# Banded attention into a squared-ReLU FFN on one core: first-batch order and idle matmuls, and the row order of the first second-layer tile

## The chip, the cores and the metric

The kernel runs on one core of one Trainium2 chip. Its engines work side by side, each through its own list of instructions in order: PE (TensorE, matrix multiplication; PEld is its weight load), DVE (VectorE) and ACT (ScalarE) for element-wise work, POOL (GpSimd), which here only issues DMA loads, and SP (SyncE), which issues stores and transposing DMAs. An engine that meets an instruction whose input isn't ready waits, and all that stands behind it in its list waits too.

The metric is device time in microseconds (us). The time of the kernel is the median of several executions; a profile shows one execution, with a span from its first to its last instruction. PEclk in a profile is the share of its full clock that TensorE was granted.

## What is computed

Eight batches of eight heads with 576 tokens and 64 channels go through causal attention within a narrow set of keys, and the 4608 rows that come out (512 wide) through a two-layer FFN whose activation is a squared ReLU.

```python
scores = (1/sqrt(64)) * q @ k^T
rel = pos[:, None] - pos[None, :]
mask_plain = (rel >= 0) & (rel < 32)                      # heads 0 to 3
mask_dil   = (rel >= 0) & (rel < 128) & (rel % 4 == 0)    # heads 4 to 7
attn = softmax(where(mask, scores, -1e9))
x = (attn @ v).transpose(0, 2, 1, 3).reshape(8 * 576, 512)
out = square(maximum(x @ w_in, 0)) @ w_out                # 512 -> 2048 -> 512
```

q, k, v and the weights arrive as float32 and are turned to bf16 by the DMAs that load them. The output is float32.

## The kernel before

**Tiles.** Heads go in four pairs, e = 0 and 1 for the plain mask, 2 and 3 for the dilated one. A batch is cut into two parts of 64 and 80 columns (times 4 residues, so 256 and 320 tokens). The attention output, transposed, lies in `xT`. The FFN takes it in tiles of 512 tokens, the first 1024 tokens as four half tiles of 256. For a half tile `ffn_groups` gives eight first-layer groups (`g1`; eight matmuls of 256 columns each, L665, then a ReLU on ACT, L676, and a square on DVE, L677) and two row blocks of four second-layer groups (`g2`; four matmuls of 512 columns each, L697). Part p of a row block needs rows of chunk p of `w_out`; after part 3 the block is copied from PSUM to an output buffer `osb` on ACT (L703; three such buffers) and stored by SP (L639). Chunk c of `w_in` serves first-layer groups 2c and 2c + 1 of each half tile.

**Buffers in PSUM.** `ps_f` ("pf") has four buffers, `ps_a` ("pa") two, `ps_o` and `ps_d` one each. A batch's transposes and scores go to "pa". The values' product and its row sums go to `po` and `pd`, or, for odd pairs of batches 0 and 1, to two "pa" buffers in part 0 and two "pf" buffers in part 1.

**The order of work** is written out by hand. `PROGRAM` (L21) is a string of codes between bars: all before the first bar runs before the first FFN group, and what stands behind bar number g + 1 runs after group g. The list `groups` gives the order of the FFN groups (L801, L802): the first layer of half tiles 0 and 1 in 16 groups, then their second layer, part by part over all four row blocks. So the four blocks hold all four "pf" buffers until part 3. The codes that matter here:

- `L0:...` a load on POOL's queue: `L0:q001` queries and keys of batch 0, part 0, pairs 0 and 1; `L0:v0d`, `L0:v0p`, `L0:v1r` values (L184, L178, L197); `L0:i0` to `i3` chunks of `w_in` (L751); `L0:o0` to `o3` chunks of `w_out` (L756). POOL issues them in order, and each waits for the transfer eight places ahead of it to land.
- `w22`, `W3`: so many idle matmuls (256 and 128 columns, L465) on a cleared tile. They compute nothing that is used.
- For batch 0, with pair e and part p: `Tep` transposes of queries and keys on PE (L493), `Cep` copies out of PSUM on DVE or ACT (L500 to L508), `Bep` the mask added by matmuls (L534), `Sep` scores (L553), `Eep` exponentials on ACT (L558), `Pep` values (L584), `Dep` row sums (L600), `Lep` and `Xep` the reciprocal by logarithm and exponential on ACT (L607, L610), `Mep` the product into `xT` on DVE (L617). In part 0 a pair of pairs shares one P, D, L, X and M step (`P20 P30`, then one `M20`).
- `z` and `y` clear buffers of later batches on DVE (L714, L715, L769, L770).
- For later batches: `1q1`, `1Q1` transposes of batch 1's queries for part 0 and part 1 with their copies (L235, L248), `1k1` keys (L252, L259), `1a1`, `1b1` scores (L304, L310, L314, L315), `1o1`, `1p1` values and outputs (L413 to L428), `1v2` spreading of values (L207).

The step that transposes in the first batch and the idle matmuls:

```python
if what == "T":
    ps = ps_a.tile([P, 1024], bf16, name="pa")
    first["T", e, part] = x = ps[:, 0 : 2 * w].rearrange("p (x r m) -> p x r m", x=2, r=RES)
    for z, nm in enumerate("qk"):
...
def turn(n: int, cols: int):
    if "W" not in first:
        pool, nm = (ps_f, "pf") if ("P", 2, 0) in first else (ps_o, "po")
        first["W"] = pool.tile([P, 512], f32, name=nm)
```

Of the kernel before, what the change touches and what calls it, by code (L numbers as in the profile page):

```python
# [12 lines left out]
RES = 4  # L13
# [6 lines left out]

PROGRAM = (  # L21
    "L0:q001 L0:q023 L0:q101 L0:q123 L0:v0d L0:v0p L0:i0 L0:v1d L0:i1 L0:v1p L0:v1r L0:i2 L0:i3 L0:o0 "
    "L1:q00123 L0:o1 L0:o2 w22 T00 C00a T10 C10a B00 B10 S00 E00 T20 C20v S10 E10 T30 C30v B20 B30 S20 E20 W3 "
    "S30 E30 W4 T01 C01v T11 C11v B01 B11 W4 S01 E01 T21 C21v W3 S11 E11 T31 C31v B21 B31 P20 P30 D20 D30 W3 "
    "S21 E21 L20 X20 W3 S31 E31 M20 W4 P00 P10 D00 D10 L00 X00 M00 | | P21 P31 D21 D31 L21 X21 M21 L31 X31 M31 "
    "| | P01 P11 D01 D11 L01 X01 M01 L11 X11 M11 | | | | | | | | | | | | z | | y L1:v0dp L0:o3 L1:q10123 "
    "L1:v1dpr | | | | L2:q00123 L2:q10123 1q1 1q3 | 1q2 | 1k2 | 1k1 1v3 | 1a2 | 1v2 1k0 1q0 | 1o2 | 1a0 1a1 | "
    "1k3 1o0 1o1 | 1a3 1Q0 | 1K0 1o3 | 1Q1 1K1 | 1Q2 | 1b0 | | 1Q3 1K2 L2:vwpdr L3:q00123 L3:q10123 | L2:x | | "
    "2q0 | | 2k0 1V2 | 1b2 1p0 | 1b1 1V3 1K3 | | 1p2 1p1 | 2a0 1b3 | 2k1 2o0 2b0 1p3 | 2q1 2k2 L3:x | | 2q2 "
    "2p0 L3:vwpdr 2a1 | | | 2b1 | 2v2 2o1 2q3 2a2 | | 2p1 | 2k3 | 2b2 2o2 | 2v3 | 2a3 2p2 L4:q10123 | 2b3 | "  # L30
    "3k1 2o3 3q1 | | 3a1 L4:q00123 2p3 | 3k0 3k2 | | 3o1 | | | 3q0 3v2 | | | | 3a0 | 3b1 3k3 | | | 3p1 L4:x "
    "3q2 L4:vwpdr | | 3b0 | 3a2 3q3 3o0 4k0 | | | 3o2 3b2 | | 3p0 3v3 | 4q1 3a3 | 3p2 4q2 4q0 | L5:q10123 3b3 "
    "| 3o3 | 4k1 | | L5:q00123 3p3 4k2 4k3 4a0 L5:vwpdr | | | 4b0 | | 4q3 | | 4o0 | | | 4a2 4v2 | 4b2 | 4a3 "
    "L5:x 4a1 | 4o2 | | | 4p2 L6:q00123 4v3 | | 4b1 | | 4p0 | | 4p1 | 5q0 5k0 | 4b3 | | | | 4o1 | | 5k2 "
    "L6:q10123 4o3 | 5q2 5k1 | | 4p3 | 5q1 |"
)

# [26 lines left out]
def kernel(  # L64
# [10 lines left out]
    P = nc.NUM_PARTITIONS  # L75
# [4 lines left out]
    bf16 = mybir.dt.bfloat16  # L80
# [20 lines left out]
    NF = DFF // P  # L101
# [9 lines left out]
    ps_f = ctx.enter_context(tc.tile_pool(name="ps_f", bufs=4, space=bass.MemoryType.PSUM))  # L111
    ps_a = ctx.enter_context(tc.tile_pool(name="ps_a", bufs=2, space=bass.MemoryType.PSUM))
# [37 lines left out]
    def staged(b: int, nm: str):  # L150


        t = rb[STAGE[b]][nm]
        return t[:, :].rearrange("p (a h x) -> p a h x", h=H, a=2)
# [47 lines left out]
    def spread_v(b: int, e: int, parts):  # L202

        p0, p1 = parts[0], parts[-1] + 1
        for hl in range(2):
            rows = slice(64 * hl, 64 * hl + 64)
            nc.vector.tensor_copy(  # L207
                vbd[b % 2][rows, e, RES * p0 : RES * p1, rows],
                vds[b][rows, e - NE // 2, p0:p1, :].rearrange("p m (r d) -> p (m r) d", d=D),
            )  # L210
# [10 lines left out]
    def trans(b: int, e: int, nm: str, part: int):  # L221

        ps = ps_a.tile([P, 1024], bf16, name="pa")
        t = staged(b, nm)
        copy = nc.scalar.copy if nm == "q" and e < NE // 2 else nc.vector.tensor_copy
        if b == 2:
            m0, n, pitch, cuts = 0, M, M, [(t[0:80, a, :, :], MS[a], 80) for a in range(2)]
        else:

            m0, n, pitch, cuts = MS[part], MN[part], 80, [(t[0:80, part, :, :], 0, 80)]  # L230
        pv_ = ps[:, 0 : 4 * pitch].rearrange("p (h c m) -> p h c m", h=2, c=2)
        for hl in range(2):
            for c in range(2):
                for src, c0, w in cuts:
                    nc.tensor.transpose(  # L235
                        pv_[:, hl, c, c0 : c0 + w], src[:, 2 * e + hl, P * c : P * c + P], ident[0:w, 0:w]
                    )
        halves(e, nm, pv_[:, :, :, 0:n], m0, n, copy)

    def halves(e: int, nm: str, t, m0: int, n: int, copy):  # L240


        for hl in range(2):
            rows = slice(64 * hl, 64 * hl + 64)
            for jj in range(2):
                src = t[64 * jj : 64 * jj + 64, hl, :, :]
                if nm == "q":
                    copy(  # L248
                        qT[rows, e, :, m0 : m0 + n].rearrange("p (c j) m -> p j c m", j=2)[:, jj, :, :], src
                    )  # L250
                elif e < NE // 2:
                    copy(  # L252
                        kbd[rows, e, m0 // 16 : (m0 + n) // 16, rows].rearrange(
                            "p i (m c j) -> p j i m c", c=2, j=2)[:, jj, :, :, :],
                        src.rearrange("p c (i m) -> p i m c", m=16),
                    )
                else:
                    x0, x1 = m0 // 64, min((m0 + n) // 64, 2)
                    copy(  # L259
                        kbd[rows, e, RES * x0 : RES * x1, rows].rearrange(  # L260
                            "p (x c j) m -> p j c x m", c=2, j=2)[:, jj, :, :, :],
                        src[:, :, 0 : 64 * (x1 - x0)].rearrange("p c (x m) -> p c x m", m=64),
                    )
                    if m0 + n == M:
                        copy(
                            kbd[rows, e, 8, rows].rearrange("p (m c j) -> p j m c", c=2, j=2)[:, jj, :, :],
                            src[:, :, n - 16 : n].rearrange("p c m -> p m c"),
                        )
# [163 lines left out]
    def step(b: int, code: str):  # L432

        what, e = code[0], int(code[1])
        part = int(what in "QKVbp")
        if what in "qk" and (b > XB or b == XB and e >= NE // 2):
            t = (qx if what == "q" else kx)[b % 2]
            by_act = what == "q" and e < NE // 2 and b < ADDED  # L440
            halves(
                e, what, t[:, 2 * e : 2 * e + 2, :, :], 0, M, nc.scalar.copy if by_act else nc.vector.tensor_copy
            )
        elif what in "qQkK":
            trans(b, e, what.lower(), part)
        elif what in "vV":
            spread_v(b, e, [part] if b in PARTED else [0, 1])
        elif what in "ab":
            scores(b, e, part)
        elif b in PARTED and e % 2:  # L450
            pv(b, e, part, *((ps_f, "pf") if part else (ps_a, "pa")))
        else:
            pv(b, e, part)

    first = {}
# [13 lines left out]
    def first_step(code: str):  # L469
# [5 lines left out]
        what, e, part = code[0], int(code[1]), int(code[2])  # L475
# [3 lines left out]
        w = RES * n  # L479
# [3 lines left out]
        def byr(ap):  # L483
            return ap.rearrange("p (r m) -> p r m", r=RES)

        if what == "T":
            ps = ps_a.tile([P, 1024], bf16, name="pa")
            first["T", e, part] = x = ps[:, 0 : 2 * w].rearrange("p (x r m) -> p x r m", x=2, r=RES)
            for z, nm in enumerate("qk"):
                t = staged(0, nm)  # L490
                for r in range(RES):
                    for hl, rows in enumerate(sides):
                        nc.tensor.transpose(  # L493
                            x[rows, z, r, :], t[0:n, part, 2 * e + hl, D * r : D * r + D], ident[0:n, 0:n]
                        )
        elif what == "C":
            copy = nc.scalar.copy if code[3] == "a" else nc.vector.tensor_copy
            x = first.pop(("T", e, part))
# [13 lines left out]
        elif what == "B":  # L512
# [11 lines left out]
            else:  # L524
                i0, x = (4, 32) if part else (3, 0)
# [9 lines left out]
        elif what == "S":  # L535
            ps = first["S", e, part]
# [3 lines left out]
            y = 0  # L540
            for x, (i, r, q0, q1) in enumerate(bl):
                z = (q1 - q0) * (RES if r is None else 1)
# [13 lines left out]
        elif what == "E":  # L556
            ps = first.pop(("S", e, part))
            nc.scalar.activation(pts[e][:, c : c + ps.shape[1]], ps, ACT.Exp, scale=SCALE)  # L558
        elif what == "P":
# [8 lines left out]
            o3, d3 = byr(o), byr(d)  # L568
            pt = pts[e]
            bl = blocks(0, e, part)  # L570
            y, dms = c, []
            for x, (i, r, q0, q1) in enumerate(bl):
                z = (q1 - q0) * (RES if r is None else 1)
# [216 lines left out]
    G = 2 * NF  # L790
# [5 lines left out]
    groups, steps = [], []  # L796
# [2 lines left out]

    head = groups[:G]  # L800
    groups[:NF] = [head[y] for y in (0, 1, 2, 3, 16, 17, 18, 19, 4, 5, 20, 21, 6, 7, 22, 23)]  # L801
    groups[NF:G] = [head[y + part] for part in range(4) for y in (8, 12, 24, 28)]  # L802
    for b in range(5, B):
        at = {"a": (-2, 8), "b": (0, 8), "o": (3, 8), "p": (6, 8), "v": (-4, 8)}
        at = {**({"k": (-9, 4), "q": (-9, 4)} if b > 5 else {}), **at}
# [50 lines left out]
```

## Time and profile before

| what | value |
|---|---|
| time, median of 8 runs | 321.14 us |
| all runs | 319.63 to 322.77 us |
| profiled execution, its time | 322.51 us |
| profiled execution, its span | 320.7 us |
| mean granted TensorE clock | 0.984 |
| PE busy | 307.5 us, 96% of the span |
| DVE busy | 201.2 us, 63% |
| ACT busy | 193.8 us, 60% |
| PE busy in 0 to 10, 20 to 30, 50 to 60, 60 to 70 us | 7.74, 7.82, 8.81, 8.11 us |
| first-layer matmul (256 columns, mean) | 326 ns over all forms |
| second-layer matmul (512 columns, mean) | 373 ns |

The profile gives, for each engine, the time in which it was busy. Matmuls are pipelined: each record is longer than the distance to the next one's start, so counts are turned into time by the distance between starts. The chain of waits follows the last instruction back to whatever released it, step by step. The list of waits sums, for each waiting instruction, how long its engine stood idle and which engine or transfer ended the wait. Where a buffer's earlier reader ended the wait, that reader is named.

### The profile page before, as it was taken

How to read it: one execution, taken by the hardware profiler on the slowest of the kernel's cores; microseconds unless marked ns; L12 is line 12 of the kernel's file. 1: busy time of each engine (PE TensorE's matmuls, PEld its weight loads, DVE VectorE, ACT ScalarE, POOL GpSimd, SP SyncE). 2: the span in 40 equal slices, each digit the busy share in tenths (PEclk: the TensorE clock that was granted, in tenths of full speed). 3: DMA queues.
4: the chain of work that ended last, by engine and by line, in shares of the span. 5: the costliest groups of instructions: out<-in, count | busy, mean ns of one | idle time of the engine just before them, and what ended most of it. 6: DMA issues, size and time to landing. Idle time of an engine off the chain costs nothing.

```text
span 320.7 us, 6834 instructions
## 1 busy us (share of the span) xinstructions
PE 307.5 (96%) x2594; PEld 191.7 (60%) x2594; DVE 201.2 (63%) x641; ACT 193.8 (60%) x416; POOL 87.3 (27%) x136
## 2 busy tenths in 40 slices
PE   7979999699999999999999999999999999999995
PEld 5758944486965555555569855555555555445543
DVE  6324578488896987997589748974897325203400
ACT  6246724676987976587468745874587456316511
POOL 8864279423426234700183032000000000000000
PEclk9589999999999999999999999999999999999999
DMA  8999999999989979998489995802200210031021
GB/s 114 159 175 192 192 163 124 206 142 164 153 88 183 172 115 179 114 181 140 64 118 126 155 128 107 157 9 64 70 1 0 68 66 2 7 91 33 2 65 65
DMA packets 79808, 34.91 MB, mean 109 GB/s; under 512 B 49824, under 2 KB 74784, under 8 KB 79776
## 3 DMA queue, kind: packets, MB, share of 16 engines
q0 software_dynamic: 47680, 18.36, 51.3%
q1 hardware_dynamic: 31952, 15.93, 25.7%
q8 instruction: 20, 0.33, 0.4%
q10 hardware_dynamic: 144, 0.20, 0.2%
q14 instruction: 12, 0.10, 0.1%
HBM read 36.90 MB, written 9.44 MB: 144 GB/s over the span
## 4 chain that ended last, share of the span: by engine, by line
PE 82%; ACT 6%; DVE 5%; DMA 4%; issue 2%; POOL 1%; SPq 0%; ACTq 0%; POOLq 0%
PE pf L665 35%; PE pf L697 34%; PE po L413 3%; PE pd L415 2%; DMA out_dram<-osb 2%; DMA kb<-in_k_dram 2%; PE pa L304 2%; ACT h2T L676 1%; PE pa L310 1%; PE pa L493 1%; DVE kbd L252 1%; ACT rec L607 1%; PE pf L553 1%; PE pf L534 1%; ACT osb L703 1%
## 5 line engine op out<-in xcount | busy, mean ns | idle before, releaser
L665 PE MATMUL pf<-xT,w_in 128*128 128x256 bf16 (+1 forms) x768 | 133.7, 326 | 2.8 <-DVE xT L617 2.5
L697 PE MATMUL pf<-w_out_sb,h2T 128*128 128x512 bf16 (+1 forms) x592 | 134.7, 373 | 0.5 <-ACT osb L703 0.5
L665 PEld LDWEIGHTS <-w_in 128*128 128x128 bf16 x768 | 82.4, 114 | 38.3 <-issue 3.7
L676 ACT ACTIVATE h2T<-pf 128x512 bf16<-128x512 f32 x144 | 83.6, 597 | 26.5 <-PE pf L665 25.7
L697 PEld LDWEIGHTS <-h2T 128*128 128x128 bf16 x592 | 54.2, 98 | 53.7 <-issue 0.7
L677 DVE TENSOR_TENSOR h2T<-h2T 128x512 bf16<-128x512 bf16 x144 | 58.0, 423 | 40.5 <-ACT h2T L676 39.0
L703 ACT COPY osb<-pf 128x512 f32<-128x512 f32 (+1 forms) x37 | 21.2, 572 | 42.5 <-PE pf L697 40.3
L178 POOL DMA_DIRECT2D vbd<-in_v_dram x40 | 28.3, 723 | 64.3 <-PE pd L415 55.1
L428 DVE TENSOR_TENSOR xT<-po,rec 128x288 bf16<-128x288 f32 (+2 forms) x52 | 23.7, 456 | 30.8 <-ACT rec L418 30.2
L417 ACT ACTIVATE rec<-pd 128x288 f32<-128x288 f32 (+2 forms) x52 | 21.5, 413 | 23.7 <-PE pd L415 22.9
L314 ACT ACTIVATE pt<-pa 128x352 bf16<-128x352 f32 (+6 forms) x56 | 27.6, 500 | 10.2 <-PE pa L310 6.3
L418 ACT ACTIVATE rec<-rec 128x288 f32<-128x288 f32 (+2 forms) x56 | 24.8, 444 | 1.8
L413 PEld LDWEIGHTS <-vbd 128*128 128x128 bf16 x286 | 17.0, 97 | 10.6 <-issue 1.3
L248 DVE COPY qT<-xx 64x288 bf16<-64x288 bf16 x80 | 20.1, 251 | 1.1
L161 POOL DMA_DIRECT2D qb<-in_q_dram x18 | 13.0, 722 | 23.7 <-DMA xx<-qb 19.9
L252 DVE COPY kbd<-xx 64x288 bf16<-64x288 bf16 x40 | 18.8, 470 | 0.6
L413 PE MATMUL po<-pt,vbd 128*128 128x96 bf16 (+3 forms) x263 | 18.0, 198 | 0.6 <-DVE xT L428 0.3
L191 POOL DMA_DIRECT2D vd<-in_v_dram x24 | 14.7, 640 | 6.8 <-DMA qb<-in_q_dram 3.7
L415 PE MATMUL pd<-pt,mk 128*128 128x96 bf16 (+5 forms) x158 | 16.3, 204 | 0.0
L161 POOL DMA_DIRECT2D kb<-in_k_dram x18 | 12.8, 713 | 0.5 <-PE pa L310 0.5
L415 PEld LDWEIGHTS <-mk 128*128 128x128 bf16 x204 | 11.6, 97 | 1.8 <-DVE kbd L252 1.1
L304 PE MATMUL pa<-qT,kbd 128*128 128x96 bf16 (+2 forms) x146 | 12.2, 201 | 0.5 <-ACT qT L248 0.5
(85 smaller groups left out, 235.9 us busy)
## 6 DMA issues: line engine op xcount, KB each, us to landing
out_dram<-osb SPq DMA_DIRECT2D x18, 128.0 KB, 3.2
qb<-in_q_dram POOLq DMA_DIRECT2D x7, 320.0 KB, 8.2
kb<-in_k_dram POOLq DMA_DIRECT2D x7, 320.0 KB, 8.7
vd<-in_v_dram POOLq DMA_DIRECT2D x32, 64.0 KB, 4.8
w_in<-in_moe_w_in_dram POOLq DMA_DIRECT2D x4, 512.0 KB, 6.9
w_out_sb<-in_moe_w_out_dram POOLq DMA_DIRECT2D x4, 512.0 KB, 10.5
qb<-in_q_dram POOLq DMA_DIRECT2D x7, 256.0 KB, 5.8
kb<-in_k_dram POOLq DMA_DIRECT2D x7, 256.0 KB, 7.1
```

The costliest lines, as they stand in the source:

```text
L161: nc.gpsimd.dma_start(t[0:n, part, hs, :], src[b, hs, t0 : t0 + RES * n, :].rearrange("h (p r) d -> p h (r d)", r=RES))
L178: nc.gpsimd.dma_start(dst[rows, e, i0:i1, rows], v[b, 2 * e + hl, 64 * i0 : 64 * i1, :].rearrange("(i p) d -> p i d", p=64),)
L314: nc.scalar.activation(pt[:, off : off + n], ps[:, 0:n], ACT.Exp, scale=SCALE)
L413: nc.tensor.matmul(oo, vb[:, e, i, :], rh, start=(x == 0), stop=(x == len(mms) - 1), skip_group_check=True)
L415: nc.tensor.matmul(dd, ones[:, :], rh, start=(x == 0), stop=(x == len(dms) - 1), skip_group_check=True)
L418: nc.scalar.activation(rec[:, 0:n], rec[:, 0:n], ACT.Exp, scale=-1.0)
L428: nc.vector.tensor_tensor(out=tok, in0=o if o is o3 else o[:, 0:n], in1=rec if o is o3 else rec[:, 0:n], op=ALU.mult)
L665: nc.tensor.matmul(acc[u][:, nt * x + y0 : nt * x + y1], w_in_sb[piece][:, kt, c0 : c0 + 509 : 4], xT[:, kt, t0 : t0 + y1 - y0], start=(kt ...
L676: nc.scalar.activation(hv, acc[u][:, :].rearrange("p (x n) -> p x n", x=per), ACT.Relu)
L677: nc.vector.tensor_tensor(out=hv, in0=hv, in1=hv, op=ALU.mult)
L697: nc.tensor.matmul(cur[m][:, c0:c1], h2[:, f, P * m : P * m + P], w_out_sb[:, f, c0:c1], start=(f == 0), stop=(f == NF - 1),)
L703: nc.scalar.copy(osb[:, c0:c1], cur[m][:, c0:c1])
```

## The change

Three edits.

1. The hand-written order of the first batch. Idle matmuls: 2 before `S00`, 3 before `S10`, 14 before the transposes of the second half's queries, 9 between those and the keys' transposes (so `T20` is split in `T20q` and `T20k`), 3 before `S20`, 3 before `S30`, 2 before `S01`, 8 at the end; those of the old order after the opening `w22` (24 in seven places) go. The value steps `P20 P30 D20 D30` and `P00 P10 D00 D10`, with their L, X and M steps, stand ahead of part-1 steps (`T21 S11 T31 S21 S31`) that they followed. The load of the last chunk of `w_out` (`L0:o3`) moves from behind batch 1's first values to right behind `L0:o2`.
2. Values of odd pairs of batches 0 and 1 that go through `pv` use two "pf" buffers in both parts.
3. The second layer of the first two half tiles goes row block by row block: all four parts of a block, then the next block. What stands between the bars of `PROGRAM` stays at the same group numbers.

```diff
 PROGRAM = (
     "L0:q001 L0:q023 L0:q101 L0:q123 L0:v0d L0:v0p L0:i0 L0:v1d L0:i1 L0:v1p L0:v1r L0:i2 L0:i3 L0:o0 "
-    "L1:q00123 L0:o1 L0:o2 w22 T00 C00a T10 C10a B00 B10 S00 E00 T20 C20v S10 E10 T30 C30v B20 B30 S20 E20 W3 "
-    "S30 E30 W4 T01 C01v T11 C11v B01 B11 W4 S01 E01 T21 C21v W3 S11 E11 T31 C31v B21 B31 P20 P30 D20 D30 W3 "
-    "S21 E21 L20 X20 W3 S31 E31 M20 W4 P00 P10 D00 D10 L00 X00 M00 | | P21 P31 D21 D31 L21 X21 M21 L31 X31 M31 "
-    "| | P01 P11 D01 D11 L01 X01 M01 L11 X11 M11 | | | | | | | | | | | | z | | y L1:v0dp L0:o3 L1:q10123 "
+    "L1:q00123 L0:o1 L0:o2 L0:o3 w22 T00 C00a T10 C10a B00 B10 W2 S00 E00 W3 S10 E10 W14 T20q W9 T20k C20v T30 "
+    "C30v B20 B30 W3 S20 E20 W3 S30 E30 T01 C01v T11 C11v B01 B11 W2 S01 E01 P20 P30 D20 D30 T21 C21v S11 L20 "
+    "X20 E11 T31 C31v M20 B21 B31 P00 P10 D00 D10 L00 X00 M00 S21 E21 S31 E31 W8 | | P21 P31 D21 D31 L21 X21 "
+    "M21 L31 X31 M31 | | P01 P11 D01 D11 L01 X01 M01 L11 X11 M11 | | | | | | | | | | | | z | | y L1:v0dp "
+    "L1:q10123 L1:v1dpr | | | | L2:q00123 L2:q10123 1q1 1q3 | 1q2 | 1k2 | 1k1 1v3 | 1a2 | 1v2 1k0 1q0 | 1o2 | "
...
         elif b in PARTED and e % 2:
-            pv(b, e, part, *((ps_f, "pf") if part else (ps_a, "pa")))
+            pv(b, e, part, ps_f, "pf")
...
         if what == "T":
-            ps = ps_a.tile([P, 1024], bf16, name="pa")
-            first["T", e, part] = x = ps[:, 0 : 2 * w].rearrange("p (x r m) -> p x r m", x=2, r=RES)
-            for z, nm in enumerate("qk"):
+            if code[3:] != "k":
+                ps = ps_a.tile([P, 1024], bf16, name="pa")
+                first["T", e, part] = ps[:, 0 : 2 * w].rearrange("p (x r m) -> p x r m", x=2, r=RES)
+            x = first["T", e, part]
+            for z, nm in [(z, nm) for z, nm in enumerate("qk") if code[3:] in ("", nm)]:
...
     groups[:NF] = [head[y] for y in (0, 1, 2, 3, 16, 17, 18, 19, 4, 5, 20, 21, 6, 7, 22, 23)]
-    groups[NF:G] = [head[y + part] for part in range(4) for y in (8, 12, 24, 28)]
+    groups[NF:G] = head[8:16] + head[24:32]
```

The rest of the order that the diff rewraps is the same on both sides.

## The prediction

> **What bounds the kernel now.** I went from the summary to the stretches in which TensorE (PE) is not full, then to the chain of waits, then to the queue that brings the weights.
>
> From 105 us on PE is busy 194.96 of 195 us, so a microsecond won before that stays won. All that the change can earn or lose lies in the first 105 us. The busy times by stretch over the start (columns: stretch, length, then busy us and instructions of PE, its weight load, VectorE (DVE), ScalarE (ACT), POOL; then granted clock, DMA share, GB/s):
>
> ```profile
> 5.13:8.54 3.41, 2.21 (x71) 1.59 (x70) 1.81 (x5) 1.99 (x7) 3.08 (x5) 1.00 1.21 149
> 8.54:11.96 3.42, 3.42 (x71) 2.43 (x63) 0.85 (x2) 1.23 (x3) 2.60 (x4) 0.50 1.46 165
> ...
> 22.20:25.61 3.41, 2.16 (x29) 1.80 (x29) 1.05 (x2) 1.47 (x4) 3.41 (x7) 1.00 1.14 171
> ```
>
> The clock is full at first, falls to half at 8.54 and comes back at 18.78. The stretch before the fall holds two PE waits: 0.35 us for a copy, and 0.85 us for the second half's keys. PE is full in the cold 10.24 us, so they cost up to 5.1 us of PE time.
>
> The chain that ended last, in order of time (start, length, what):
>
> ```profile
> 31.75 8.80 PE pf L665 x79
> ...
> 43.11 1.02 DVE vbd L715
> ...
> 53.47 0.88 PE pf L697 x4
> 54.35 0.02 issue
> 54.37 0.58 ACT osb L703
> ...
> 55.60 6.53 DMA out_dram<-osb
> ...
> 62.23 0.59 ACT osb L703
> ...
> 64.36 1.31 PE pf L665 x12
> ```
>
> After the first layer of the first two half tiles (L665) the chain runs through DVE's clearing and copies for batch 1, and then through a store: all four row blocks of the second layer end together, three output buffers are full, and the fourth copy waits for a store of 6.53 us. What waits of PE and ACT there (waiter, what it waited for, total, times, longest):
>
> ```profile
> PE pa L415 <- DVE kbd L252: 1.0, 1, 1.0
> PE pa L235 <- DVE xT L428: 0.6, 1, 0.6
> PE pa L415 <- DVE kbd L259: 0.5, 1, 0.5
> ...
> ACT osb L703 <- DMA out_dram<-osb: 2.0, 1, 2.0
> ```
>
> Three of these are waits for one of the two "pa" buffers, which values and transposes share. The weights' queue, in POOL's timeline, and the time from issue to landing of the four w_out chunks (least, median, most):
>
> ```profile
> 24.49 1.14 POOL L756 DMA_DIRECT2D w_out_sb<-in_moe_w_out_dram  x2
> 25.58 1.27 POOL L184 DMA_DIRECT2D vd<-in_v_dram  x2
> ...
> 36.95 0.56 POOL L756 DMA_DIRECT2D w_out_sb<-in_moe_w_out_dram  x1 [1.58 <-DMA w_out_sb<-in_moe_w_out_dram]
> 40.58 0.74 POOL L161 DMA_DIRECT2D qb<-in_q_dram  x1 [3.07 <-DMA w_out_sb<-in_moe_w_out_dram]
> DMA to landing us min/median/max: 7.4/10.5/15.2
> ```
>
> Chunk 1 lands just before 36.95 (it releases that issue), chunk 2 at 25.05 + 15.2 = 40.3, and chunk 3 at 36.95 + 7.4 = 44.4. In the old order PE needs chunk 3 only at 53.
>
> **The change, step by step.** All sums are against the profiled execution: span 320.7 us, time 322.51, so 1.8 us lie around the span. That run is one of the slower of the eight (319.63 to 322.77, median 321.14).
>
> *Idle matmuls.* 44 of 128 columns instead of 24 after the opening 22. Their starts are 56 ns apart at full clock (three at 18.82 take 0.33 us, of which 0.22 is one matmul's own length), so 20 more are 1.1 us of PE. W14 and W9 stand around the transposes of the second half's queries: 23 x 56 ns = 1.3 us in place of a wait of 0.85, so the keys' transposes start near 8.9 instead of 8.30. Nobody behind them minds, as the next step shows. In the stretch that preceded the fall, PE gains about 1.0 us of full 128 x 128 streaming, so I expect the clock to hold at 8.54.
>
> *Values ahead of the second part.* P20 P30 D20 D30 now stand ahead of T21. They need the values issued at 6.31 and 6.90, landing 5.1 to 5.8 us later (12.4). Behind that wait in PE's queue stand T21 and S11, for which E11 on ACT and C21 on DVE wait. P00 P10 need pieces that land at 10.13 + 4.6 = 14.7. L20 X20 (0.59 + 0.63 us) move ahead of E11, and L00 X00 ahead of E21 and E31; P11 and P21 that use these stand after the first FFN groups. On a warm clock PE then reaches the first FFN group when the outputs of the first two pairs are in xT (M20, M00), about 17.5, instead of 22.13. But right after two groups comes P21, which needs the last values: issued 17.15 and 17.76, landing 4.9 to 5.3 us later, 22.6. So PE waits some 3 us there, and the clock may well fall in that wait. Two groups more (16 x 109 ns = 1.75 us), then 3.2 us until the last product of batch 0, as before (28.53 to 31.7), then the same 79 matmuls of 8.7 us: the first layer ends near 37.3 with a full clock and near 39 with one half-clock stretch. Before it ended at 40.4. So this part is worth 1.4 to 3.1 us at that point, bounded by transfers and not by PE.
>
> *Row blocks, and chunk 3 of w_out earlier.* The first row block now needs chunk 2 in its third part and chunk 3 in its fourth. On POOL's queue chunk 3 moves past six value transfers of batch 1 (two vd of 64 KB, four vbd of 32 KB, 256 KB in all), to right behind chunk 2. At the 209 GB/s of 34 to 37 us a chunk of 512 KB takes 2.5 us. Both chunks after 36.7 give 41.6; I take 41.8. The bounds are 41.3, and the 44.4 of before if the earlier place in the queue buys nothing. The six value transfers land up to 2.5 us later (near 43.5), for readers after 47. PE does parts 0 and 1 at once, waits for chunk 2 (39.1 to 40.3), waits for chunk 3, and ends the block at 41.8 + 0.87 = 42.7. At the same amount of work the old order stood at 40.38 + 4 x 0.865 = 43.84. So of the 1.4 to 3.1 us only 1.1 survive. This wait has a use: DVE's 5.5 us of clearing (41.81 to 47.35) starts earlier and is over when the first batch-1 transposes come, at 42.7 + 1.73 = 44.4.
>
> *From there to the sixth matmul group of the third half tile.* Before, PE needed 43.84 to 65.5 (12 matmuls from 64.20) = 21.7 us. Eight waits lie in it: 0.15, 0.16, 0.18, 0.52, 0.40, 0.26, 0.99 and 0.61 = 3.3 us. Each also uncovers the tail of the matmul before it, 0.17 us (four L697 take 1.03 us but the next starts after 0.86), 1.4 us together; pure work is 17.0. The row blocks store one after another, so ACT's 2.0 us behind the store go. Values of odd heads take "pf" buffers in both parts, and row blocks leave those free, so the "pa" waits go too. What stays by my count: 0.3 for query copies on ACT (four of 259 ns against one part of 0.87), 0.15 for spread values, 0.2 for scores, and 0.5 before the second group of the third half tile, whose "pf" waits for ACT's last output copy and logarithm (0.58 + 0.38). That is 1.15 us. PE arrives at 42.7 + 17.0 + 1.15 = 60.85 instead of 65.5: 4.65 us. The bounds: no such wait left and chunk 3 at 41.3 gives 6.3; all waits left and chunk 3 at 44.4 gives -1.5.
>
> *After 66 us.* The transposing DMAs on SP's queue stood behind the nine stores (54.98 to 64.1). The last stores now issue near 58.5, so they follow the shift, and DVE is busy 34.1 of the 40 us from 80 to 120, so it can follow. I leave 0.15 for what is given back. Span 320.7 - 4.5 = 316.2, time **318.0 us**.
>
> [...] The row: the clock fell after a stretch with 2.21 us busy, mostly 64 x 64 tiles, and stayed after one with 2.16 us of mostly full tiles, so a wait far shorter than 3.4 us can cost the clock. [...] I go by the row.
>
> **The rivals.**
> 1. *The clock falls in the w_out wait (slower).* If PE idles more than about 2 of 3.4 us around 38 to 42, the clock halves as at 8.54. For it: two waits with one part of 0.87 us between them. Against: if the clock fell already at P21, PE comes later and waits less than 1.5 us. One stretch of 3.41 us costs 1.7 (319.7). It decides the sign if it lasts three stretches, as it did from 8.54 to 18.78: 5.1 us, 323.1. Chance 14 in 100.
> 2. *DVE, not the buffers, is behind the waits.* The releasers named are DVE copies, and DVE works without a break from 47.37 to 53. Then only the 1.1 us and the 0.6 of the store survive: 320.8. Against: DVE now starts that work 3 us earlier. Chance 17.
> 3. *Chunk 3 lands as late as before.* 2.6 us later than taken: 320.6. For it: the transfers overlap (256 KB of values land within 1.6 us after chunk 2, so they shared the engines). Against: 52 GB/s from 42 to 43 show an idle queue. Chance 14.
> 4. *The idle matmuls don't hold the clock.* Then PE reaches P21 near 24 and the w_out wait still sets the pace: 318.0 to 318.6. One in three, inside the forecast.
>
> **How the numbers follow.** The forecast (317 to 319.5) has 55 in 100. What a measurement can tell from no change is about 0.5%, 1.6 us: faster is below 319.5, slower above 322.7. Faster: 55 + 5 from better ends of rivals 2 and 3 = 60. Slower: rival 1, and 2 from the worst of rival 3 = 16. The rest, 24, is no change. The range goes from 316.3 (all waits gone, 322.5 - 6.2) to 322.4, which takes in rivals 2 and 3 and the short form of rival 1; about 6 lie below and 14 above.
>
> **What would show it.** Right: a granted clock of 1.00 from 5 to 17 us; a PE wait at P21 until about 22.6; the fourth part of the first row block at 41.8 behind a w_out transfer; no "pa" wait behind L428 or L252 before 65; no ACT wait for a store; the first matmul of the third half tile near 57. Wrong: a clock of 0.50 after 39 us, chunk 3 beyond 43, or DVE copies releasing PE at 46 to 53 as before.

## The result, and the profile after

| | before | after |
|---|---|---|
| median of all runs | 321.53 us (32 runs, 319.57 to 323.47) | 317.07 us (11 runs, 316.07 to 319.61) |
| profiled execution, time / span | 322.51 / 320.7 us | 316.07 / 314.3 us |
| mean granted clock in it | 0.984 | 1.000 |

The ratio of after to before is 0.9871, with a 95% interval of 0.9845 to 0.9896: 4.5 us less by the medians. The two profiled executions differ by 6.4 us; the one of before lies 1.0 us above its median, the one of after is the fastest of its runs. Lines of the FFN and of the first batch stand two further down in after (L665 is L667, L697 is L699, L703 is L705, L584 is L586).

The stretches of after at the start (columns as before: stretch, length, then busy us and instructions of PE, its weight load, DVE, ACT, POOL; granted clock, DMA share, GB/s):

```profile
5.13:8.54 3.41, 2.75 (x70) 2.17 (x63) 1.81 (x5) 2.40 (x8) 3.08 (x5) 1.00 1.17 138
8.54:11.96 3.42, 3.42 (x101) 2.79 (x98) 0.91 (x3) 0.77 (x2) 2.59 (x4) 1.00 1.52 179
20.96:24.37 3.41, 2.08 (x46) 1.81 (x41) 0.49 (x2) 1.32 (x4) 2.94 (x5) 1.00 1.20 181
```

PE's busy time in the first stretch rose from 2.21 to 2.75 us and the clock didn't fall behind it. The third stretch holds the new wait for the last values, and the clock stayed there too, in this execution. The waits of PE in the first 70 us of after (waiter, what it waited for, total, times, longest):

```profile
PE po L586 <- DMA vbd<-in_v_dram: 1.3, 1, 1.3
PE pf L699 <- DMA w_out_sb<-in_moe_w_out_dram: 1.2, 1, 1.2
...
PE pf L667 <- DVE xT L619: 0.9, 2, 0.6
PE po L586 <- DMA vd<-in_v_dram: 0.7, 1, 0.7
...
PE pf L667 <- ACT osb L705: 0.2, 1, 0.2
```

All "pa" waits behind values and `xT` are gone, and so is ACT's wait for a store. The two longest waits that are left before 45 us, apart from the opening, are for transfers; products into `xT` (0.9 us) and a copy (0.5 us) stand beside them. The chain that ended last says the same (start, length, what):

```profile
24.11 1.05 POOL w_out_sb L758 x2
25.16 15.88 DMA w_out_sb<-in_moe_w_out_dram
41.05 0.04 issue
41.09 2.75 PE pf L699 x12
...
56.26 0.59 ACT osb L705
56.90 0.82 PE pf L667 x6
57.71 0.29 PE pa L235 x8
58.00 1.31 PE pf L667 x12
```

Chunk 3 of `w_out` is issued at 25.16 and lands at 41.05, and PE goes on 0.04 us later. The last line is the group that stood at 64.36 in the chain of before: 6.36 us earlier, and the spans differ by 6.4. So the whole difference of the profiled executions arises before this point, and none of it is given back behind it (from 105 to 300 us PE is busy 194.97 of 195.00 us).

The second layer begins at 37.11 in after and at 40.38 in before, 3.27 us earlier. The wait for chunk 3 costs 1.23 of that, and at the end of the first row block's worth of matmuls 1.9 us are left (41.09 + 0.86 = 41.95 against 43.84). The other 4.5 us are won between there and 59 us, where before had its eight waits.

### The profile page after: what moved, and what is told of

Its sections match the earlier page's. It is cut to its first block, busy times and chain, and to the rows that moved or that the text cites. A ratio compares the mean times of both kernels' runs of the same rounds, so it can differ in the third digit from the quotient of the medians.

```text
span 314.3 us, 6875 instructions
## 1 busy us (share of the span) xinstructions
PE 302.9 (96%) x2614; PEld 190.2 (61%) x2614; DVE 200.6 (64%) x641; ACT 193.7 (62%) x416; POOL 87.2 (28%) x136
## 4 chain that ended last, share of the span: by engine, by line
PE 79%; DMA 9%; ACT 4%; POOL 3%; issue 2%; DVE 1%; ACTq 0%; POOLq 0%
PE pf L699 37%; PE pf L667 33%; DMA w_out_sb<-in_moe_w_out_dram 5%; PE po L413 3%; PE pd L415 2%; DMA w_in<-in_moe_w_in_dram 2%; DMA vd<-in_v_dram 2%; PE pa L304 2%; PE pa L310 1%; ACT qT L248 1%; ACT h2T L678 1%; POOL qb L161 1%; POOL kb L161 1%; PE pa L235 1%; ACT rec L417 1%
## 5 line engine op out<-in xcount | busy, mean ns | idle before, releaser
L699 PE MATMUL pf<-w_out_sb,h2T 128*128 128x512 bf16 (+1 forms) x592 | 134.8, 373 | 1.7 <-DMA w_out_sb<-in_moe_w_out_dram 1.2
L667 PE MATMUL pf<-xT,w_in 128*128 128x256 bf16 (+1 forms) x768 | 133.9, 326 | 1.5 <-DVE xT L619 0.9
L667 PEld LDWEIGHTS <-w_in 128*128 128x128 bf16 x768 | 82.4, 113 | 37.0 <-issue 2.4
L699 PEld LDWEIGHTS <-h2T 128*128 128x128 bf16 x592 | 54.2, 98 | 55.1 <-issue 2.2
L705 ACT COPY osb<-pf 128x512 f32<-128x512 f32 (+1 forms) x37 | 21.2, 572 | 45.8 <-PE pf L699 45.8
L178 POOL DMA_DIRECT2D vbd<-in_v_dram x40 | 28.2, 720 | 57.8 <-PE pd L415 49.4
L428 DVE TENSOR_TENSOR xT<-po,rec 128x288 bf16<-128x288 f32 (+2 forms) x52 | 23.7, 456 | 31.5 <-ACT rec L418 31.0
L417 ACT ACTIVATE rec<-pd 128x288 f32<-128x288 f32 (+2 forms) x52 | 21.5, 413 | 23.9 <-PE pd L415 23.1
L161 POOL DMA_DIRECT2D qb<-in_q_dram x18 | 13.0, 722 | 19.9 <-DMA xx<-qb 17.2
L197 POOL DMA_DIRECT2D vbd<-in_v_dram x16 | 9.7, 615 | 10.9 <-PE pd L415 7.4
```

Source lines behind the costliest of these rows:

```text
L161: nc.gpsimd.dma_start(t[0:n, part, hs, :], src[b, hs, t0 : t0 + RES * n, :].rearrange("h (p r) d -> p h (r d)", r=RES))
L178: nc.gpsimd.dma_start(dst[rows, e, i0:i1, rows], v[b, 2 * e + hl, 64 * i0 : 64 * i1, :].rearrange("(i p) d -> p i d", p=64),)
L417: nc.scalar.activation(rec[:, 0:n], d[:, 0:n], ACT.Ln)
L428: nc.vector.tensor_tensor(out=tok, in0=o if o is o3 else o[:, 0:n], in1=rec if o is o3 else rec[:, 0:n], op=ALU.mult)
L667: nc.tensor.matmul(acc[u][:, nt * x + y0 : nt * x + y1], w_in_sb[piece][:, kt, c0 : c0 + 509 : 4], xT[:, kt, t0 : t0 + y1 - y0], start=(kt ...
L699: nc.tensor.matmul(cur[m][:, c0:c1], h2[:, f, P * m : P * m + P], w_out_sb[:, f, c0:c1], start=(f == 0), stop=(f == NF - 1),)
```

## The experiments

Theory at the start: each of the three parts of the change earns something. First rival: the order of the first batch earns all, since the clock no longer falls. Second rival: the row blocks with their two helpers ("pf" buffers, early chunk 3) earn all. Every kernel was timed against before on the same chip; intervals are 95%.

### The parts, each alone

**e1_order_only**: the new first-batch order and idle matmuls alone.

```diff
-... L0:o1 L0:o2 L0:o3 w22 ...      | z | | y L1:v0dp L1:q10123 ...
+... L0:o1 L0:o2 w22 ...            | z | | y L1:v0dp L0:o3 L1:q10123 ...
-            pv(b, e, part, ps_f, "pf")
+            pv(b, e, part, *((ps_f, "pf") if part else (ps_a, "pa")))
-    groups[NF:G] = head[8:16] + head[24:32]
+    groups[NF:G] = [head[y + part] for part in range(4) for y in (8, 12, 24, 28)]
```

> The first batch's new order and idle matmuls alone; the last w_out chunk, the part-by-part second layer and the pv buffers as before. My theory (each edit frees something the others do not): the first layer ends near 37.1 instead of 40.4 when the clock would have fallen, but the copies of batch 1, the pa waits and the store wait stay, so 319.3 us, near the lowest runs of before (319.6). Rival A (the clock and the order are the whole gain): 317.1, as the changed kernel. Rival B (the order is worth nothing because transfers set the pace): 321.5.

Measured: 320.46 us, ratio 0.9982 (0.9959 to 1.0006), 1.2 us above what was expected. In its profile the clock held at 8.54 but was half from 24.59 to 28.00, behind a wait of 2.1 us for the last values, so the first layer ended at 39.24 and not near 37.1. **e8_idle_only** adds the first four groups of new idle matmuls (2, 3, 14 and 9) to before, which keeps its own 24; it also has `S10 E10` ahead of `T20`, and `T20` split, as in after. The values stay where they were.

```diff
-... B00 B10 S00 E00 T20 C20v S10 E10 T30 C30v B20 B30 S20 E20 ...
+... B00 B10 W2 S00 E00 W3 S10 E10 W14 T20q W9 T20k C20v T30 C30v B20 B30 S20 E20 ...
```

> The kernel before with the new idle matmuls ahead of the second half's transposes (2, 3, 14 and 9) and nothing else. Theory of the clock: the granted clock does not fall near 8.5 us, the first layer ends near 37.5 in every execution, and all later waits stay: 319.7 us, with a narrower spread than before. Rival (the clock at the start is worth nothing): 321.2.

Measured: 320.77 us, ratio 0.9975 (0.9957 to 0.9992), 1.1 us above what was expected. Its profile is of the slowest of its twelve executions; the clock is 1.00 throughout, and the first layer ends 1.7 us earlier than in before, at 38.65. But the waits behind it (same columns) take most of that back:

```profile
ACT osb L705 <- DMA out_dram<-osb: 3.0, 1, 3.0
...
PE pa L235 <- ACT rec L417: 1.0, 1, 1.0
...
PE pa L235 <- DVE xT L428: 1.0, 2, 0.6
PE pa L415 <- DVE kbd L252: 1.0, 1, 1.0
```

ACT's wait for a store grew from 2.0 to 3.0 us (the store itself takes 7.51 us here, 6.53 in before), the waits behind L417 and L428 from 0.6 to 2.0. The 12 matmuls of the third half tile start at 63.28, only 0.9 us earlier than in before. In e1 it is the same (2.7 us for the store). A faster start ran into the part-by-part second layer.

**e2_rows_only**: row blocks, "pf" buffers and early chunk 3 with the old first-batch order.

```diff
-... L0:o3 w22 T00 C00a T10 C10a B00 B10 W2 S00 E00 W3 S10 E10 W14 T20q W9 T20k ...
+... L0:o3 w22 T00 C00a T10 C10a B00 B10 S00 E00 T20 C20v S10 E10 T30 ...
```

> Row blocks, pf buffers for odd pairs and the early last w_out chunk, with the old order of the first batch. My theory: the first row block ends at 43.9 instead of 42.0 when the clock has fallen, since the first layer then ends at 40.4, and as in the changed kernel when it has not; all waits behind it are gone as in the changed kernel: 318.0 to 318.5 us, with a wider spread than the changed kernel. Rival A (clock and order are the whole gain): 321.5. Rival C (row blocks are the whole gain): 317.1.

Measured: 317.03 us, ratio 0.9883 (0.9848 to 0.9919), which is after's own, as rival C had it. PE's timeline (start, length, what; in brackets the idle time before it and what ended it):

```profile
40.03 1.02 PE L697 MATMUL pf<-w_out_sb,h2T 128*128 128x512 bf16 x4 [0.55 <-DMA w_out_sb<-in_moe_w_out_dram]
42.46 2.75 PE L697 MATMUL pf<-w_out_sb,h2T 128*128 128x512 bf16 x12 [1.41 <-DVE qb L769]
```

The second wait is named after a clearing on DVE that ended at 42.42; chunk 3 of `w_out` landed at 42.42 too. The profiled execution kept a full clock without a single new idle matmul, so the fall at 8.54 in before is not fixed to the order: it happens in some executions and not in others (mean granted clock 0.983 to 1.000 in the six runs of e2).

**e3_no_idle**: after with none of the new idle matmuls (the opening 22 stay).

```diff
-... B00 B10 W2 S00 E00 W3 S10 E10 W14 T20q W9 T20k C20v ... S31 E31 W8 | ...
+... B00 B10 S00 E00 S10 E10 T20 C20v ... S31 E31 | ...
```

> The changed kernel without any idle matmul but the opening 22. Theory of the clock: the granted clock falls to 0.50 near 8 us in most executions, PE reaches the last values late, the first layer ends 1 to 3 us later, and the w_out wait of 1.2 us hides a part: 318.2 us. Rival (the idle matmuls hold nothing that counts, w_out sets the pace): 317.1. Rival (the held clock is most of the gain): 320 or more.

Measured: 316.48 us, ratio 0.9864 (0.9836 to 0.9891). In its profile one half-clock stretch lies in the wait for the last values (21.90 to 25.32), the first layer ends 1.1 us later than in after (38.17), and the wait for chunk 3 shrinks from 1.2 to 0.4 us: it lands at 41.32, and PE goes on at 41.37, against 41.09 in after.

```profile
41.37 2.75 PE L698 MATMUL pf<-w_out_sb,h2T 128*128 128x512 bf16 x12 [0.44 <-DMA w_out_sb<-in_moe_w_out_dram]
```

**So the second rival holds:** the row edit with its two helpers earns all that can be measured. Order and idle matmuls earn nothing on top of it that these intervals can tell: in the profiles of e2, e3 and after PE waits for the last chunk of `w_out`, however early it gets there.

### Inside the row edit

**e4_o3_late**: after with chunk 3 back behind batch 1's first values.

```diff
-... L0:o2 L0:o3 w22 ...    | y L1:v0dp L1:q10123 ...
+... L0:o2 w22 ...          | y L1:v0dp L0:o3 L1:q10123 ...
```

> The changed kernel with the last w_out chunk in its old place on POOL's queue, behind six value transfers. My theory: it lands near 43.7 instead of 41.05 and PE waits that much longer in the first row block: 319.7 us. Rival (the place in the queue buys nothing, the transfers share the engines anyway): 317.1.

Measured: 319.64 us, ratio 0.9951 (0.9920 to 0.9981). PE's timeline (columns as in e2):

```profile
39.58 2.88 PE L699 MATMUL pf<-w_out_sb,h2T 128*128 128x512 bf16 x12
45.52 2.75 PE L699 MATMUL pf<-w_out_sb,h2T 128*128 128x512 bf16 x12 [3.06 <-DMA w_out_sb<-in_moe_w_out_dram]
```

Chunk 3 lands at 45.48, 4.09 us behind chunk 2; in after it is 2.44 us (38.61 to 41.05). So the late place costs 1.65 us, about what the six value transfers between them take (41.39 to 42.99). The distance is much the same in all profiles: 2.42 to 2.58 us in the nine with chunk 3 right behind chunk 2, 3.91 to 4.09 in the five with the late place. The other 2.8 us in this profile lie ahead of it: chunk 2 too landed at 41.39 instead of 38.61. By the medians the early place is worth 317.07 against 319.64, 2.6 us, or 0.8% by the ratios. What makes up the 1 us beyond the 1.65 is not shown.

**e5_pa**: after with the old "pa" buffers for the odd pairs' values of part 0.

```diff
-            pv(b, e, part, ps_f, "pf")
+            pv(b, e, part, *((ps_f, "pf") if part else (ps_a, "pa")))
```

> The changed kernel with odd pairs' values of part 0 back in two pa buffers. Theory of the buffers: the waits of 0.5 and 1.0 us for pa buffers around 1o1 and 1o3 come back, with the uncovered matmul tails 1.5 to 2.0 us: 318.8 us. Rival (the order of the rows and the spaced stores are the whole gain, the buffers cost nothing): 317.0.

Measured: 319.13 us, ratio 0.9935 (0.9901 to 0.9969). PE's waits between 40 and 62 us:

```profile
PE pa L415 <- DVE kbd L252: 1.0, 1, 1.0
PE pa L415 <- DVE kbd L259: 0.6, 1, 0.6
PE pa L235 <- DVE xT L428: 0.4, 1, 0.4
PE pa L413 <- ACT qT L248: 0.3, 1, 0.3
```

Before had the same four waits (one of them named after a load), here 2.3 us together; DVE's and ACT's work is that of after, and only the buffers differ. **e9_clear_early** asks from the other side: before with its 5.5 us of clearing on DVE early, `z` ahead of the first FFN group and `y` behind the fourth.

```diff
-... L00 X00 M00 | | P21 ... M11 | | | | | | | | | | | | z | | y L1:v0dp ...
+... L00 X00 M00 z | | P21 ... M11 y | | | | | | | | | | | | | | L1:v0dp ...
```

> The kernel before with DVE's clearing for batches 1 and 2 moved from behind the first layer to two earlier places where DVE is idle (behind M00 and behind M11). Theory (several causes behind the old waits): the waits on DVE copies from 46.9 to 53 go, about 1.0 us with tails; the pa waits and the store wait stay: 320.0 us. Rival (DVE's late clearing is behind all of them): 317.5. Rival (it is behind none, the buffers are): 321.0.

Measured: 320.75 us, ratio 0.9961 (0.9936 to 0.9986), 0.75 us above what was expected. DVE is free 5.5 us earlier, and still the "pa" waits of 1.0, 0.5, 0.4 and 0.3 us stay, and the store wait with 2.1. So DVE's late start was worth some 0.4% (0.1% to 0.6%), and the two shared buffers are the reason for the "pa" waits: with other buffers (after) they vanish, with a free DVE (e9) they don't, although the releaser's name is a DVE copy.

The two losses, 0.8% without the early chunk and 0.65% without the buffers, add up to about the 1.3% of the whole, each uncertain by some 0.4%. Row blocks with neither were not run. If the losses add, they would earn next to nothing, but that is an estimate, and what the spaced stores earn by themselves was not measured.

### A version that gets past the wait for w_out

**v1_pair_clear**: after with the clearing early (as in e9) and the first two row blocks interleaved, so that chunks 0 and 1 are used by both blocks before chunk 2 is needed.

```diff
-    groups[NF:G] = head[8:16] + head[24:32]
+    groups[NF:G] = [head[y] for y in (8, 12, 9, 13, 10, 11, 14, 15)] + head[24:32]
-... M00 S21 E21 S31 E31 W8 | | P21 ... M11 | | | | | | | | | | | | z | | y ...
+... M00 S21 E21 S31 E31 W8 z | | P21 ... M11 y | | | | | | | | | | | | | | ...
```

> The changed kernel with the clearing moved early in the same way, and the first two row blocks interleaved (parts 0 and 1 of both, then parts 2 and 3 of the first, then of the second) so that PE has work while the last w_out chunks are on their way. Theory (the w_out wait and the uncovered tails at its two ends are all that the row blocks cost, 1.2 to 1.4 us): 315.7 us. Rival (something else then ends last, a load of batch 1 or DVE): 317.0.

Measured: 316.91 us, ratio 0.9846 (0.9815 to 0.9876): no better than after within the intervals, and 1.2 us above what was expected. The wait for `w_out` is gone from the profile, but the clock fell in the wait for the last values (half from 23.94 to 27.35), and the second layer begins only at 38.56.

**v2_pair_clear_values** moves the last values of batch 0 ahead of chunk 1 of `w_in` too, and part 2 of the second block ahead of part 3 of the first (below against v1); **e10_values_first** is after with that load order alone.

```diff
-... L0:v0p L0:i0 L0:v1d L0:i1 L0:v1p L0:v1r L0:i2 ...
+... L0:v0p L0:i0 L0:v1d L0:v1p L0:v1r L0:i1 L0:i2 ...
-    groups[NF:G] = [head[y] for y in (8, 12, 9, 13, 10, 11, 14, 15)] + head[24:32]
+    groups[NF:G] = [head[y] for y in (8, 12, 9, 13, 10, 14, 11, 15)] + head[24:32]
```

> The kernel after with three edits: DVE's clearing ahead of the first FFN groups, the first two row blocks of the second layer interleaved (so that each w_out chunk has twice the work before the next is needed), and the last values of the first batch ahead of w_in chunk 1 in the queue. Theory (the wait for those values and then the w_out chunks set the pace up to 41 us): the wait at P21 of 1.3 us goes, the first layer of the first two half tiles ends near 36, the w_out wait stays under 1 us, and with the pace before it gone the time is about 315, some 2 us below the kernel after. Rival (w_in and w_out, which now stand later in the queue, set the pace whatever stands ahead): a wait for w_in chunk 1 or a longer one for w_out takes the place, third half tile no earlier than 55.8 us, time 316.5 to 317.5.

> The kernel after with one edit: the last values of the first batch ahead of w_in chunk 1 in POOL's queue; clearing and row blocks as in after. Theory (in after the landing of w_out chunk 3 sets the pace, so an earlier first layer buys nothing by itself): the P21 wait of 1.3 us moves to a w_in wait, the first layer ends near 36, but the first row block still resumes at 41 to 42 and the w_out waits grow from 1.2 to 2.5 us or more; third half tile at 55.5 to 57, time 317, ratio 0.987. Rival (the values were the pace, and the pairing of row blocks is idle): 315.1, ratio 0.981, as the version with all three edits.

Measured: v2 315.09 us, ratio 0.9807 (0.9773 to 0.9841); e10 317.63 us, ratio 0.9880 (0.9839 to 0.9920). PE's timeline in v2:

```profile
23.03 1.94 PE L667 MATMUL pf<-xT,w_in 128*128 128x256 bf16 x16 [1.48 <-DMA w_in<-in_moe_w_in_dram]
...
28.03 8.78 PE L667 MATMUL pf<-xT,w_in 128*128 128x256 bf16 x79 [0.30 <-DVE xT L619]
36.65 5.34 PE L699 MATMUL pf<-w_out_sb,h2T 128*128 128x512 bf16 x23
```

and PE's waits in e10 from 30 to 46 us:

```profile
PE pf L699 <- DMA w_out_sb<-in_moe_w_out_dram: 2.0, 2, 1.6
```

In both the wait for values became a wait for `w_in`, of 1.5 and 2.1 us, as v2's rival had it for that place; but in v2 the second layer begins at 36.65 and runs without a break, its chunk 3 landing at 41.44, just ahead of the seventh group of four matmuls, which needs it, while e10 waits 2.0 us for the same chunks (42.10) and is no faster than after. For v2 the theory's time held, and the rival's wait for `w_in` came too without setting the pace; for e10 the theory's time and the wait held in the main, with 2.0 us where 2.5 were expected. But its first layer ended at 37.22 and not near 36, and behind a cold stretch that the expectation did not have (42.23 to 45.64) the third half tile began at 58.90, not at 55.5 to 57. Loads without pairing (e10) and pairing with early clearing but without the loads (v1) gain nothing clear of noise over after. Loads and pairing without the early clearing were not run, so the clearing's share in v2 is open.

**c_after_again** is after unchanged, on v2's chip.

> The kernel after once more, unchanged, beside the version above on the same chip. Theory: 317.1 as before, ratio 0.987; the profile has the w_out wait of about 1.2 us whether or not the clock falls in the wait at P21. Rival (its time depends on which of the two clocks a run draws): the profile with a half-clock stretch comes out 1.5 us or more longer than the 314.3 us span without.

Measured: 317.19 us, ratio 0.9867 (0.9828 to 0.9906), 2.1 us above v2. Its profile had a half-clock stretch in the wait for the last values and a span of 315.5 us, 1.2 more than the profile of after with a full clock, which is between theory and rival; its wait for `w_out` was 0.8 us. Chunk 3 explains the 1.2 us: it lands 1.08 us later (42.13 against 41.05), and PE goes on 0.04 us after it in both.

**e11_best_no_idle**: v2 without the new idle matmuls.

```diff
-... B00 B10 W2 S00 E00 W3 S10 E10 W14 T20q W9 T20k C20v ... S31 E31 W8 z | ...
+... B00 B10 S00 E00 S10 E10 T20q T20k C20v ... S31 E31 z | ...
```

> The version with early clearing, paired row blocks and values ahead of w_in chunk 1, without the idle matmuls of the first batch (the opening 22 stay). Here no w_out wait hides what the start loses. Theory (idle matmuls hold nothing that matters): at most one half-clock stretch more than with them, time 315 to 316, ratio 0.981 to 0.984. Rival (they hold the clock, and their worth was only hidden behind the w_out wait): a half clock before 20 us or in several stretches, first layer of the first two half tiles 1.7 us or more later than 36.7, time 316.8 or more.

Measured: 314.89 us, ratio 0.9801 (0.9767 to 0.9834), the fastest here: its slowest execution (315.52) is below the fastest of after (315.70, in c_after_again). The profiled execution had a half clock from 13.29 to 20.11, as the rival said, and its second layer starts 1.3 us later than v2's (37.92); it was the slowest of this kernel's six runs (315.52), and v2's profiled one the fastest of its six (314.08). By the medians, the idle matmuls earn nothing here either, where no wait for `w_out` could hide their worth. Another wait can hide a part: the one for chunk 1 of `w_in` is 1.5 us in v2's profile and 0.5 in e11's.

## Why the prediction came out as it did

The time was right (317.07 against 318.0, range 316.3 to 322.4), and the place where it comes from too: the row blocks with their buffers and the early chunk. That the 4.5 us of gain are also the distance of the medians is luck in part. The sum stood on a profiled execution 1.0 us above its median, and the profiled execution of after lies 1.0 us below its own, so these two differ by 6.4 us: between them the sum is 1.9 us short.

| step | predicted | profile of after |
|---|---|---|
| first FFN group | 17.5 | 18.15 |
| wait at P21, end of it | some 3 us, 22.6 | 1.33 us, 22.53 |
| first layer ends | 37.3 (39 with a cold stretch) | 37.1 (38.6 in c_after_again, with one) |
| chunk 3 lands | 41.8 (41.3 to 44.4) | 41.05 |
| first row block ends | 42.7 | 41.95 (41.09 + 0.86) |
| from there to the end of the sixth group of the third half tile | 18.15 | 17.2 (to 59.15) |
| given back behind it | 0.15 | none |
| span | 316.2 | 314.3 |

*Idle matmuls.* The clock held at 8.54 as forecast, but the term that the cold 10.24 us "cost up to 5.1 us of PE time" was mis-sized for the time of the kernel. e8's profile has no cold time, and e8 won 0.8 us by the medians; e3 and e11 left the idle matmuls out and lost nothing. Nor are they shown to be what held the clock there: of the five profiles without the new ones (before, e2, e3, e9, e11) only before's fell at that place, and with them the clock still fell in the wait for the last values in the profiles of e1, e4, e5, v1 and c_after_again. Rival 4, kept inside the forecast at one in three, is near to what the runs show: the forecast could do without this part. One reading ahead of it was wrong: the clock is not full at first. In before the 256-column idle matmuls at the opening start 213 ns apart until 5.08 us, those of the first layer 109 ns apart, and the trace's record of the clock begins at 5.13. So the stretch that ended at 8.54 was the first at full clock.

*Values ahead of the second part.* The bound was right (transfers, not PE): P21 ended at 22.53. The wait was smaller than 3 us because P20 had waited 0.7 us for its own values (the later of them landed at 13.75, not at 12.4) and the first FFN group 0.6 us for M00's product in `xT`, so that PE came later, and because 16 of P21's matmuls ran ahead of the wait. Of the 1.1 us that were let "survive" the medians show nothing: e2, with the old order, has after's time. Without the row edit the part and the idle matmuls together give 0.2% (e1, none to 0.4%), as the gain goes into the store wait and the waits behind it.

*Row blocks and chunk 3.* This step carried the forecast, and its two terms measured apart are 2.6 us (e4) and 2.1 us (e5). The landing was taken 0.75 us too late for the profiled execution (in c_after_again chunk 3 landed at 42.13). The 1.15 us of waits that were to stay are 0.4: 0.15 to 0.2 for the copies of queries, and 0.21 for ACT's output copy instead of 0.5; spread values and scores cost nothing.

*The rivals.* Rival 1 (the clock falls in the wait for `w_out`) did not happen in after, where PE was busy 2.75 of the 3.98 us from 37.11 to 41.09. In e10's profile it did: the clock halved from 42.23 to 45.64, right behind the two waits (2.00 of 3.41 us idle), and that span is 317.7, 2.2 us above c_after_again's 315.5 with the same landing of chunk 3. So one stretch cost some 2 us there, against the 1.7 of the rival, but the median of e10 is after's: three stretches, from which it would decide the sign, were seen there in no profile. Those 2.00 us are the rival's own mark; below it the profiles go both ways: 1.20 us of 3.41 were idle ahead of the fall in before and 1.87 ahead of one in e1, while 1.87 in e4 and 1.33 in after cost no clock. Rival 2 (DVE is behind the waits) falls with e5 and e9. Rival 3 (chunk 3 as late as before) had the price right: 2.6 us, measured in e4.

## What to carry to other kernels

Before warming a clock or moving work forward, find the next transfer that the work meets, and ask at what time it lands whatever the engines do; a gain ahead of it is worth only what the wait behind it leaves (in e3 the first layer ended 1.1 us later than in after, and PE went on 0.28 us later behind the wait for chunk 3). A landing can be moved by the issue's place in the queue (1.65 us in e4), and the need for it by the order in which tiles use it: here earlier values and paired row blocks each earned nothing clear of noise on top of after, and both together, with the early clearing, some 0.6% by the medians. When a list of waits names copies on a busy engine, ask which buffer the waiting instruction needs: here other buffers took these waits away (2.3 us in e5, gone in after), and an engine that was free 5.5 us earlier did not (e9).

## What the runs showed of the hardware

*The clock falls without a long idle time.* The half-clock stretches within the spans last 3.41 us (v1, e10) or two or three times that (6.83 in e11, 10.24 in before). Some windows of 3.41 us on full clock, from profiles of the kernels named (the last column but one is the share of the window in which columns streamed through the array, worked out from each matmul's start and its columns, at 216 ns for 512 columns, the distance between starts of second-layer matmuls on full clock in before). The edges are reckoned on in steps of 3.41 us from the last change of the clock, an estimate from the lengths of those stretches:

| window | PE busy, us | longest wait in it, us | share streaming | clock behind it |
|---|---|---|---|---|
| before, 5.13 to 8.54 | 2.21 | 0.85 | 0.45 | half, 10.24 us |
| e11, 9.87 to 13.29 | 2.09 | 0.51 | 0.36 | half, 6.83 us |
| v1, 20.53 to 23.94 | 1.67 | 1.74 | 0.37 | half, 3.41 us |
| e10, 38.82 to 42.23 | 1.41 | 1.55 | 0.32 | half, 3.41 us |
| e4, 40.91 to 44.33 | 1.55 | 1.87 of 3.06, cut by the window's end | 0.37 | full |
| after, 20.96 to 24.37 | 2.08 | 1.33 | 0.47 | full |

The lines of e11, whose second stretch is cold (columns as in the first fence):

```profile
9.87:13.29 3.42, 2.09 (x51) 1.44 (x51) 1.35 (x4) 0.65 (x2) 2.45 (x4) 1.00 1.26 129
13.29:16.70 3.41, 3.34 (x63) 2.51 (x64) 0.84 (x3) 1.79 (x3) 2.91 (x6) 0.50 1.05 149
```

The length of one wait doesn't decide: waits of half a microsecond came before a fall in e11, and 3.06 us in e4 cost no clock (by these edges it falls into two windows, with PE busy 1.55 and 2.22 us). Ahead of the four falls in the table PE was busy for 1.41 to 2.21 us of the window. The share of the window does better, though it doesn't part them cleanly. In the first 100 us of all fourteen profiles the clock fell eleven times, ten of them behind a window of 0.37 or less, and the lowest shares that it survived are 0.37 and 0.42. The exception is the fall of before, at 0.45 with mostly 64 x 64 tiles; what makes the clock fall there is not shown.

*Landings differ between profiles by as much as the place in the queue moves them.* Chunk 2 of `w_out`, at the same place of the same queue, landed at 38.61 in after, 39.70 in c_after_again, 39.52 in e10 and 41.39 in e4, with issues between 23.01 and 25.46; the first two are the same kernel and differ by 1.1 us, and the late place moved chunk 3 by 1.65. Where PE waits for such a landing, a single profile doesn't give the worth of an edit; the medians do.
